# Loading a batch's first pairs ahead of w2, summing a mean on TensorE part by part, spreading the statistics and halving the last store

## The chip, the cores and the metric

The kernel runs on one core of one Trainium2 chip. The metric is device time in microseconds (us). Before: 585.83 us, median of 3 runs (585.38 to 586.06). A profile is one execution; its span is about 1.8 us shorter than the device time of the same execution. Every run also lists its mean granted clock of TensorE (1.0 is full clock).

Names: PE is TensorE, DVE VectorE, ACT ScalarE, POOL GpSimd, SP SyncE. "xT" is the attention output transposed, "xc" the same minus its mean, "ps" the first FFN product, "o_ps" the second, "sc" the scores, "av_ps" attention times v.

## The reference

```python
# q, k, v: (8 batches, 12 heads, 448 tokens, 64); w1: 768 x 3072; w2: 3072 x 768
scores = scale * np.matmul(q, k.transpose(0, 1, 3, 2))
attn = np.maximum(scores, 0.0) ** 2 / S
x = np.matmul(attn, v)                       # then heads side by side: (8, 448, 768)
mu = mean(x); var = mean((x - mu) ** 2)
xn = (x - mu) / sqrt(var + 1e-6) * g_ln
out = x + np.maximum(xn @ w_ch1, 0.0) @ w_ch2
```

## The kernel before

Heads are worked in 6 pairs per batch, numbered through from zero (pair 12 is the first of batch two; some of the expectations say "batch one" for batch zero). Batches zero and one are transposed on PE. From batch two on the transposes of q and k are DMA transposes from the SP queue; q, k, v and the weights come through the POOL queue, which casts to bf16. Batches are taken two by two: FFN one of both, then FFN two of both, with the next batches' attention steps spread between. "warm" matmuls on constant data keep PE busy in the first batch, where there is no FFN to fill it.

```python
def load_paired(b):
    alloc_batch(b)
    for a in range(NPAIR):
        load_pair(b, a)                       # q, q, k, k: 56 KB each
        if a == 1:
            load_heads(b, [("v", 0, H)])      # 672 KB

def att_AV(i, half=None):
    ...
    nc.vector.tensor_scalar(xT_of(b, pr), ps, c2, None, op0=Alu.mult)
    if pr == 1:
        nc.vector.tensor_add(xs[b], xT_of(b, 0), xT_of(b, 1))
    elif 1 < pr < NPAIR - 1:
        nc.vector.tensor_add(xs[b], xs[b], xT_of(b, pr))

def center(b):
    mean_ps = ps_m.tile([P, S], fp32, tag="m")
    nc.tensor.matmul(mean_ps, ones, xs[b], start=True, stop=False)
    nc.tensor.matmul(mean_ps, ones, xT_of(b, K1 - 1), start=False, stop=True)
    ...
    for ki in range(K1):
        nc.vector.tensor_sub(xc_t[:, ki, :], xT_of(b, ki), mean_ps)

def first_end():                              # end of batch zero
    att_AV(NPAIR - 1, 0)
    att_T(NPAIR, evac=False)
    warm_up(4)
    att_AV(NPAIR - 1, 1)
    warm_up(8)
    center(0)
    att_T_out(NPAIR)
...
        for c in range(W2C):                  # order of the POOL queue, after w1
            load_w2(c)                        # 4 x 1152 KB
        load_paired(2)
```

## Time and profile before

| what | value | where |
|---|---|---|
| device time, span | 585.83 us, 583.8 us | runs, page |
| PE busy | 563.6 us | busy times |
| longest wait of PE | 8.9 us, one time | waits |
| from 93 to 578.9 us | PE without a gap | chain of waits |
| last matmul to the end of the span | 4.94 us | timeline |

The waits of PE in the kernel before (who waited for whom, total us, times, longest us):

```profile
PE sc L209 <- DMA qkT_t<-k_sb: 8.9, 1, 8.9
PE ps L290 <- DVE xc_t L257: 1.8, 7, 0.7
```

The chain of work that ended last, around that wait. The profiler follows it back from the last instruction, at each step to what released it (start us, us, what):

```profile
71.23 1.26 PE ps L290 x6
72.48 1.07 SPq L177
...
73.67 7.69 DMA qkT_t<-k_sb
81.36 0.04 issue
81.40 1.00 PE sc L209 x4
82.40 2.35 PE ps L290 x6
...
86.83 2.38 PE ps L290 x12
```

PE stands from 72.5 to 81.4 us for the k transpose of pair 12. The two rows after it are slow: six FFN matmuls take 2.35 us, while later twelve take 2.38. The stretches of ten us (busy time of each engine, granted clock, DMA share, GB/s) show why:

```profile
10.00:20.00 10.00, 9.81 (x108) 4.34 (x105) 9.60 (x18) 9.93 (x13) 5.26 (x7) 1.00 1.37 201
20.00:30.00 10.00, 8.28 (x70) 3.81 (x69) 9.93 (x17) 8.09 (x10) 9.96 (x6) 1.00 1.37 201
...
70.00:80.00 10.00, 2.47 (x18) 0.87 (x14) 3.46 (x10) 2.57 (x4) 6.49 (x9) 0.80 1.49 141
80.00:90.00 10.00, 8.60 (x40) 3.41 (x41) 3.41 (x6) 5.15 (x7) 6.26 (x9) 0.69 2.29 134
```

After the length of the stretch the columns are PE, PEld (weight loads), DVE, ACT, POOL, then the granted clock, the DMA share and GB/s. The clock is 0.69 from 80 to 90 us. From 10 to 30 us DVE (third) is nearly full, and ACT (fourth) from 10 to 20. The end of batch zero on DVE (start us, us, engine, line, what, idle before and its releaser):

```profile
29.57 0.61 DVE L242 TENSOR_SCALAR xT_t<-av_ps 128x448 bf16<-128x448 f32 x1
30.21 0.98 DVE L246 TENSOR_TENSOR xs_t<-xs_t,xT_t 128x448 bf16<-128x448 bf16 x1
31.12 0.61 DVE L212 TENSOR_TENSOR at<-at 112x896 bf16<-112x896 bf16 x1
32.20 0.62 DVE L242 TENSOR_SCALAR xT_t<-av_ps 128x448 bf16<-128x448 f32 x1 [0.47 <-PE av_ps L235]
33.56 3.28 DVE L257 TENSOR_TENSOR xc_t<-xT_t,mean_ps 128x448 bf16<-128x448 bf16 x6 [0.73 <-PE mean_ps L253]
```

The mean addition of 0.98 us stands in front of the last squaring (L212), on which AV and the mean hang.

### The profile page before, as it was taken

What the parts mean: (1) busy time and instruction counts of PE and PEld (TensorE: products, weight loads), DVE (VectorE), ACT (ScalarE), POOL (GpSimd) and SP (SyncE); (2) the same over time, 40 slices, a digit from 0 to 9 for tenths busy, and PEclk for the clock granted to TensorE, in tenths of its full rate; (3) what the DMA queues carried; (4) which work ended last, traced back from release to release, by engine and by line L of the source; (5) the groups of instructions that cost most, each with busy time, mean ns of one, the idle gap of its engine ahead of it and who ended that gap; (6) DMA issues with size and microseconds to landing.
All of it is one profiled execution on the core that took longest, in us unless ns stands there. A gap on an engine that the chain in (4) does not pass through costs nothing.

```text
span 583.8 us, 8969 instructions
## 1 busy us (share of the span) xinstructions
PE 563.6 (97%) x3542; PEld 287.3 (49%) x3542; DVE 263.6 (45%) x505; ACT 266.7 (46%) x392; POOL 143.3 (25%) x188
## 2 busy tenths in 40 slices
PE   8989949999999999999999999999999999999996
PEld 5444414445555444445555544445555544556663
DVE  4977814284544334375444424256454334401111
ACT  6937825672233576663232475664313364440000
POOL 7793170163006500074003610074000000000000
PEclk9999969999999999999999999999999999999999
DMA  9999999299218933599125954299223141000121
GB/s 181 201 205 210 195 145 129 38 116 96 71 44 105 154 36 58 78 111 104 44 71 66 169 54 80 47 95 112 54 58 73 47 71 33 0 2 28 55 54 55
DMA packets 153242, 51.79 MB, mean 89 GB/s; under 512 B 125808, under 2 KB 149616, under 8 KB 153200
## 3 DMA queue, kind: packets, MB, share of 16 engines
q0 software_dynamic: 90144, 25.50, 45.3%
q1 hardware_dynamic: 62576, 25.25, 22.0%
q8 instruction: 28, 0.46, 0.3%
q10 hardware_dynamic: 480, 0.46, 0.3%
q14 instruction: 14, 0.11, 0.1%
HBM read 51.91 MB, written 11.01 MB: 108 GB/s over the span
## 4 chain that ended last, share of the span: by engine, by line
PE 90%; DVE 5%; DMA 2%; ACT 1%; issue 0%; SPq 0%; ACTq 0%
PE o_ps L306 38%; PE ps L290 37%; PE sc L209 7%; PE av_ps L235 6%; DVE at L212 2%; ACT at L211 1%; DMA qkT_t<-k_sb 1%; DVE xc_t L257 1%; DMA h_114<-in_q_dram 1%; DVE qkT_t L201 1%; DVE xT_t L242 0%; DVE xs_t L246 0%; PE tp_ps L190 0%; PE mean_ps L253 0%; PE mean_ps L252 0%
## 5 line engine op out<-in xcount | busy, mean ns | idle before, releaser
L290 PE MATMUL ps<-xc_t,w_112 128*128 128x448 bf16 x1152 | 230.1, 354 | 1.8 <-DVE xc_t L257 1.8
L211 ACT ACTIVATE at<-sc 112x896 bf16<-112x896 f32 x192 | 165.0, 915 | 138.1 <-PE sc L209 137.6
L306 PE MATMUL o_ps<-w_113,h_114 128*128 128x384 bf16 x1344 | 225.6, 326 | 0.0
L212 DVE TENSOR_TENSOR at<-at 112x896 bf16<-112x896 bf16 x192 | 120.2, 632 | 184.2 <-ACT at L211 184.2
L306 PEld LDWEIGHTS <-h_114 128*128 128x128 bf16 x1344 | 128.6, 98 | 95.0 <-issue 12.2
L290 PEld LDWEIGHTS <-w_112 128*128 128x128 bf16 x1152 | 108.7, 98 | 115.6 <-issue 18.8
L292 ACT ACTIVATE h_114<-ps 128x448 bf16<-128x448 f32 x192 | 104.6, 545 | 110.6 <-PE ps L290 110.3
L112 POOL DMA_DIRECT2D q_sb<-in_q_dram x72 | 50.3, 703 | 213.1 <-DMA qkT_t<-q_sb 114.8
L309 DVE SCALAR_TENSOR_TENSOR o_t<-o_ps,rstd_t,x_t 128x384 f32<-128x384 f32 x56 | 34.5, 616 | 82.1 <-PE o_ps L306 82.1
L209 PE MATMUL sc<-qkT_t 64*112 64x448 bf16 x384 | 59.8, 378 | 10.3 <-DMA qkT_t<-k_sb 8.9
L112 POOL DMA_DIRECT2D k_sb<-in_k_dram x72 | 50.2, 701 | 38.8 <-DMA v_sb<-in_v_dram 26.2
L235 PE MATMUL av_ps<-at,v_sb 112*64 112x448 bf16 x384 | 47.3, 361 | 1.0 <-DVE at L212 0.6
L209 PEld LDWEIGHTS <-qkT_t 64*112 64x112 bf16 x384 | 18.4, 126 | 46.4 <-issue 34.3
L257 DVE TENSOR_TENSOR xc_t<-xT_t,mean_ps 128x448 bf16<-128x448 bf16 x48 | 26.2, 614 | 16.2 <-PE mean_ps L253 16.2
L242 DVE TENSOR_SCALAR xT_t<-av_ps 128x448 bf16<-128x448 f32 x48 | 29.6, 617 | 3.6 <-PE av_ps L235 3.6
L235 PEld LDWEIGHTS <-v_sb 112*64 112x64 bf16 x384 | 17.6, 109 | 24.7 <-issue 18.3
L159 POOL TENSOR_SCALAR w_112<-w_112,g_sb 128x512 bf16<-128x512 bf16 x12 | 20.8, 1744 | 1.3 <-DMA w_112<-in_moe_w_ch_dram 1.3
L284 DVE BATCH_NORM_STATS2 stats<-x_t 128x6 f32<-128x384 bf16 x28 | 15.2, 542 | 0.0
L283 DVE BATCH_NORM_STATS2 stats<-x_t 128x6 f32<-128x384 bf16 x28 | 14.6, 523 | 0.0
L327 PE MATMUL w_ps<-w_113,ones 128*128 128x256 bf16 x70 | 11.4, 304 | 1.2 <-DVE w_113 L77 1.2
L279 DVE RECIPROCAL rstd_t<-rstd_t 128x7 f32<-128x7 f32 x4 | 0.8, 201 | 22.5 <-ACT rstd_t L278 22.5
L246 DVE TENSOR_TENSOR xs_t<-xs_t,xT_t 128x448 bf16<-128x448 bf16 x24 | 10.0, 416 | 0.8
(36 smaller groups left out, 81.0 us busy)
## 6 DMA issues: line engine op xcount, KB each, us to landing
v_sb<-in_v_dram POOLq DMA_DIRECT2D x7, 672.0 KB, 10.0
w_112<-in_moe_w_ch_dram POOLq DMA_DIRECT2D x6, 768.0 KB, 25.8
w_113<-in_moe_w_ch_dram POOLq DMA_DIRECT2D x4, 1152.0 KB, 19.1
q_sb<-in_q_dram POOLq DMA_DIRECT2D x72, 56.0 KB, 4.1
k_sb<-in_k_dram POOLq DMA_DIRECT2D x72, 56.0 KB, 4.1
out_dram<-o_t SPq DMA_DIRECT2D x8, 336.0 KB, 2.8
out_dram<-o_t SPq DMA_DIRECT2D x8, 288.0 KB, 2.6
out_dram<-o_t SPq DMA_DIRECT2D x8, 240.0 KB, 2.6
```

The lines of the kernel that those rows point to most:

```text
L112: nc.gpsimd.dma_start(by_pair[:, a, :, x, :], src[b, 2 * a + x].rearrange("(p j) d -> p j d", j=NJ))
L159: eng.tensor_scalar(w, w, g_sb[:, ki:ki + 1], None, op0=Alu.mult)
L209: nc.tensor.matmul(sc[:SP, hh, :S], qkT[i][r, 1, t * SP:(t + 1) * SP], qkT[i][r, 0, :], start=True, stop=True)
L211: nc.scalar.activation(at, sc[:SP, :, :S], Act.Relu)
L212: nc.vector.tensor_mul(at, at, at)
L235: nc.tensor.matmul(ps[hh * D:(hh + 1) * D, :], v_sb[:, 2 * pr + hh, t * D:(t + 1) * D], attn[i, t][:, hh, :], start=(t == 0), stop=(t == N ...
L242: nc.vector.tensor_scalar(xT_of(b, pr), ps, c2, None, op0=Alu.mult)
L257: nc.vector.tensor_sub(xc_t[:, ki, :], xT_of(b, ki), mean_ps)
L290: nc.tensor.matmul(ps, w1[:, ki, ni * P:(ni + 1) * P], xc[u * U + bb][:, ki, :], start=(ki == 0), stop=(ki == K1 - 1))
L292: nc.scalar.activation(h1[:, ni, bb * S:(bb + 1) * S], ps, Act.Relu)
L306: nc.tensor.matmul(o_sb[1], h1[:, ki, m * P:(m + 1) * P], w2[:, ki, j * hd:(j + 1) * hd], start=(ki == 0), stop=(ki == K2 - 1))
L309: nc.vector.scalar_tensor_tensor(o_sb[0][:, j * hd:(j + 1) * hd], o_sb[1], rstd[u][:, m:m + 1], x_tok[u][:, m, j * hd:(j + 1) * hd], op0=A ...
```

## The change

Four parts with different aims: get pair 12 and 13 in before w2, so that PE needn't stand; take the additions for batch zero's mean off DVE, with PE summing part by part in place of warm-up matmuls; run the statistics every second FFN block over the last 14, in place of every block of the last 7; and store the last tile in two column halves, so that less is left after the last matmul.

```diff
-    def load_paired(b):
-        alloc_batch(b)
-        for a in range(NPAIR):
+    def load_paired(b, a0=0, a1=NPAIR):
+        if a0 == 0:
+            alloc_batch(b)
+        for a in range(a0, a1):
...
+        if b == 0:
+            return                            # no additions on DVE for batch zero
         if pr == 1:
             nc.vector.tensor_add(xs[b], xT_of(b, 0), xT_of(b, 1))
...
+    def mean_part(ki):
+        if ki == 0:
+            mean0_ps = ps_f.tile([P, S], fp32, tag="f")
+            mean0[0] = mean0_ps
+        nc.tensor.matmul(mean0[0], ones, xT_of(0, ki), start=(ki == 0), stop=(ki == K1 - 1))
...
+            last = u == NU - 1 and m == MU - 1
-            if j == 1:
+            if j == 1 or last:
+                d0, d1 = (j * hd, (j + 1) * hd) if last else (0, d_model)
...                                           # store columns d0:d1
-        warm_up(4)
+        if i > 1:
+            mean_part(i - 2)
+            warm_up(2)
+        else:
+            warm_up(4)
...                                           # first_end: the same, mean_part(NPAIR - 2)
-                if bb == 1 and ni >= K2 - MU:
-                    items.append((0.0, lambda u=u, m=ni - (K2 - MU): ffn_stats(u, m)))
+                m = (ni - (K2 - 2 * MU)) // 2
+                if bb == 1 and m >= 0 and ni % 2 == 0:
+                    items.append((0.0, lambda u=u, m=m: ffn_stats(u, m)))
...
+        load_paired(2, 0, 2)
         for c in range(W2C):
             load_w2(c)
-        load_paired(2)
+        load_paired(2, 2)
```

More of the change, by code (lines that the diff above doesn't have):

```diff
@@ L43 @@
     MU = UT // P
+    NU = B // U
     assert SP * NJ == S and MU * P == UT
@@ L226, in att_AV @@
                 xT[b // U] = xT_t
-            xs_t = xs_pool.tile([P, S], bf16, tag="xs")
-            xs[b] = xs_t
+            if b > 0:
+                xs_t = xs_pool.tile([P, S], bf16, tag="xs")
+                xs[b] = xs_t
         if half != 1:
@@ L248 @@
     xc = {}
-    def center(b):
-        mean_ps = ps_m.tile([P, S], fp32, tag="m")
-        nc.tensor.matmul(mean_ps, ones, xs[b], start=True, stop=False)
+    mean0 = {}
+    def mean_part(ki):
[3 more added lines that the diff above has]
+        nc.tensor.matmul(mean0[0], ones, xT_of(0, ki), start=(ki == 0), stop=(ki == K1 - 1))
+    def center(b):
+        if b == 0:
+            mean_ps = mean0[0]
+        else:
+            mean_ps = ps_m.tile([P, S], fp32, tag="m")
+            nc.tensor.matmul(mean_ps, ones, xs[b], start=True, stop=False)
         nc.tensor.matmul(mean_ps, ones, xT_of(b, K1 - 1), start=False, stop=True)
@@ L318, in ffn_2 @@
                     nc.sync.dma_start(
-                        out_tok[u * U + bb, c0 - g0 * SP:c1 - g0 * SP, jj, :],
-                        o_sb[0][c0 - m * P:c1 - m * P, :])
+                        out_tok[u * U + bb, c0 - g0 * SP:c1 - g0 * SP, jj, d0:d1],
+                        o_sb[0][c0 - m * P:c1 - m * P, d0:d1])
                     c0 = c1
@@ L367, in step_fine @@
         att_QK(i, 3)
-        warm_up(4)
+        if i > 1:
+            mean_part(i - 2)
+            warm_up(2)
+        else:
+            warm_up(4)
     def first_end():
@@ L372, in first_end @@
         att_T(NPAIR, evac=False)
-        warm_up(4)
+        mean_part(NPAIR - 2)
+        warm_up(2)
         att_AV(NPAIR - 1, 1)
@@ L398, in steps_of @@
         return done_at[b]
-    NU = B // U
     segs = []
```

## The prediction

> **What bounds it now.** TensorE is busy 563.6 of 583.8 us (busy times). Its waits sum to 14.8 us, 8.9 of them one wait of the score matmul (L209) for the DMA transpose of k. From 93 to 578.9 us the chain of waits is TensorE without a gap. Three places can give time:
>
> 1. **Stall at 72.5 to 81.4 us (chain, timeline).** Batch two's first q/k loads queue behind w2: w2 lands at 54.5 to 71.5 us, the pairs at 71.9 to 74.5 (issue records); the transposes are issued at 72.3 and 73.7 and land at 76.9 and 81.4, the second slowed by the v load. Then the granted clock is 0.69 for 80 to 90 us (windows): six FFN matmuls took 2.35 us in place of 1.24, four score matmuls 1.00 in place of 0.52; with the next groups about 2.2 us. [...] At stake: 11.1 us.
> 2. **First batch, 8 to 33 us.** The chain is on VectorE (DVE), busy 9.6 and 9.9 of 10 us in 10-20 and 20-30. On it: four mean additions (three of 0.39 us, one 0.98; 2.15 together) and the first mean matmul (0.19).
> 3. **Tail.** Last matmul ends 578.9; DVE 0.62; last store landed 582.7; end 583.8.
>
> **What the change does.**
> - *Loads.* Pairs 12, 13 and v go ahead of w2. From the queue's rates (w1 landed at 48.9; pairs 150 KB/us, v 180, w2 207) I estimate pairs landed by 51, v 56, w2 78, the rest 86. w2 is first used at about 113 then, pair 14 at 91: room for both. Pair 12's transposes are then issued when the program reaches them, at about 56.5, needed at about 70, but beside w2. Beside v they took 7.3 to 10.4 us, alone 2.4. ([...] the trace shows the transposes nearly silent for 3.5 us while v was served.) w2's pieces take 131 ns against 61, so I estimate landing at 65 to 72: a stall of 0 to 3 us remains, about 1. Gain about 10.
> - *Mean.* Four DVE additions leave the chain; five matmuls of 0.19 us replace ten warm-up matmuls of about 0.12 in TensorE's slack. ScalarE idled 1.25 us before its last activation there, but DVE is the longer: gain about 2.2.
> - *Statistics spread.* No TensorE wait comes from them: 0.
> - *Store by halves.* The final store carries half; from 2.8 us to landing, about 0.5.
>
> Sum: about 12.9 us. **Predicted 572.9 us, 8 in 10 between 571.0 and 576.5; faster by over 2% 0.68, within 2% 0.31, slower 0.01.**
>
> **What would show each step.** (1) The 8.9 us wait gone or under 3; granted clock 0.95 or more from 70 to 90 us; w2 landing at 72 to 79. (2) First FFN matmul at about 31.9 in place of 34.2. (3) TensorE waits unchanged around the statistics. (4) Last matmul to end 4.4 us in place of 4.9.
>
> **What would make it wrong.** Transposes starved for all of w2 (clock drop again: 577 to 580). ScalarE binding in the first batch (gain 1). Statistics ahead of the sixth x transpose's landing, blocking DVE and then TensorE. A PSUM wait because the running mean holds one of two "f" buffers.

Passages that no trace or run of this case shows are cut out of it, and out of the expectations of "changed, again" and "four warm-ups" below, where marked. About 10 for the loads, 2.2 for the mean, 0 and about 0.5 come to 12.7, and "about 12.9" was recorded (585.8 less 572.9).

## The result

The changed kernel took 572.41 us (572.13 to 573.27, 4 runs) against 585.82 us (4 runs). The ratio is 0.9774, 95% interval 0.9758 to 0.9791. A ratio here is the mean time of one kernel's fast runs over that of the other's in the same rounds, so it is not quite the ratio of the medians quoted. The ratio is clear of 2% here and when the kernel ran a third time; in the second (0.9781, interval up to 0.9801) it just isn't.

The longest waits of PE in the changed kernel; the wait for the k transpose is gone:

```profile
PE ps L306 <- DVE xc_t L273: 1.8, 7, 0.7
PE w_ps L345 <- DVE w_113 L78: 1.2, 1, 1.2
PE tp_ps L192 <- DVE xT_t L245: 0.7, 1, 0.7
```

The timeline of PE where it stood before, and that of the SP queue which issues pair 12's and 13's transposes:

```profile
70.44 1.31 PE L306 MATMUL ps<-xc_t,w_112 128*128 128x448 bf16 x6
71.68 0.58 PE L211 MATMUL sc<-qkT_t 64*112 64x448 bf16 x4
72.20 1.31 PE L306 MATMUL ps<-xc_t,w_112 128*128 128x448 bf16 x6
```

```profile
58.22 1.29 SPq L179 DMA_TRANSPOSE qkT_t<-q_sb  x1
59.62 1.24 SPq L179 DMA_TRANSPOSE qkT_t<-k_sb  x1
64.14 1.19 SPq L179 DMA_TRANSPOSE qkT_t<-q_sb  x1
65.44 1.30 SPq L179 DMA_TRANSPOSE qkT_t<-k_sb  x1
```

The transposes are issued at 58.2 and 59.6 us in place of 72.3 and 73.7. By the issue records they land at 67.5 and 71.6 us, the second 0.06 us before the score matmul that needs it starts. The stretches:

```profile
20.00:30.00 10.00, 9.19 (x89) 4.10 (x88) 8.86 (x15) 7.57 (x9) 9.97 (x6) 1.00 1.37 201
30.00:40.00 10.00, 8.38 (x51) 3.52 (x51) 6.91 (x13) 2.85 (x5) 8.83 (x7) 0.83 1.30 206
70.00:80.00 10.00, 9.84 (x60) 4.45 (x57) 7.72 (x16) 7.14 (x11) 1.40 (x2) 1.00 1.17 203
80.00:90.00 10.00, 9.85 (x58) 4.47 (x57) 4.08 (x8) 6.80 (x11) 5.47 (x8) 1.00 1.51 149
```

From 70 to 90 us the clock is full now. But it is 0.83 between 30 and 40 us, where it was 1.00 in the profile of before. On DVE the end of batch zero now reads:

```profile
27.75 0.61 DVE L245 TENSOR_SCALAR xT_t<-av_ps 128x448 bf16<-128x448 f32 x1
28.29 0.61 DVE L214 TENSOR_TENSOR at<-at 112x896 bf16<-112x896 bf16 x1
30.06 0.62 DVE L245 TENSOR_SCALAR xT_t<-av_ps 128x448 bf16<-128x448 f32 x1 [1.16 <-PE av_ps L238]
31.22 3.28 DVE L273 TENSOR_TENSOR xc_t<-xT_t,mean_ps 128x448 bf16<-128x448 bf16 x6 [0.54 <-PE mean_ps L269]
```

The addition is gone, but DVE now waits 1.16 us for AV, where it waited 0.47.

To compare many profiles I read three marks from each trace: A, the start of the first score matmul; B, the start of the sixth matmul of the first FFN group (the last one to wait for centring); C, the end of the last matmul. All in us:

| kernel | A | B | A to B | B to C | C to end |
|---|---|---|---|---|---|
| before | 7.13 | 36.89 | 29.76 | 541.96 | 4.94 |
| changed | 6.83 | 34.55 | 27.71 | 532.74 | 4.21 |

So this pair of profiles gives 2.3 us up to B, 9.2 us from B to C (with the halved clock near 35 us in it) and 0.7 us in the tail: 12.3 us, the difference of the spans (583.8 less 571.5). The first two were then tested by runs; the tail was only read from the traces. The last PE row of each timeline, before and changed, ends at 578.85 and 567.28 us:

```profile
574.79 4.06 PE L306 MATMUL o_ps<-w_113,h_114 128*128 128x384 bf16 x24
565.82 1.46 PE L322 MATMUL o_ps<-w_113,h_114 128*128 128x384 bf16 x8
```

### The profile page after: what moved, and what is told of

It reads as the page before. It is cut to its first block, busy times and chain, and to the rows that moved or that the text cites. A ratio compares the mean times of both kernels' runs of the same rounds, so it can differ in the third digit from the quotient of the medians.

```text
span 571.5 us, 8962 instructions
## 1 busy us (share of the span) xinstructions
PE 562.1 (98%) x3536; PEld 286.4 (50%) x3536; DVE 261.8 (46%) x501; ACT 266.1 (47%) x392; POOL 144.4 (25%) x188
## 4 chain that ended last, share of the span: by engine, by line
PE 93%; DVE 4%; ACT 2%; DMA 1%; issue 0%; SPq 0%; ACTq 0%
PE o_ps L322 39%; PE ps L306 38%; PE sc L211 8%; PE av_ps L238 7%; ACT at L213 2%; DVE at L214 1%; DVE xc_t L273 1%; DMA h_114<-in_q_dram 1%; PE tp_ps L192 0%; DVE qkT_t L203 0%; DVE xT_t L245 0%; PE w_ps L345 0%; PE mean_ps L269 0%; PE mean_ps L268 0%; DVE o_t L325 0%
## 5 line engine op out<-in xcount | busy, mean ns | idle before, releaser
L325 DVE SCALAR_TENSOR_TENSOR o_t<-o_ps,rstd_t,x_t 128x384 f32<-128x384 f32 x56 | 34.5, 616 | 82.1 <-PE o_ps L322 82.1
L345 PE MATMUL w_ps<-w_113,ones 128*128 128x256 bf16 x60 | 10.0, 303 | 1.2 <-DVE w_113 L78 1.2
L102 POOL DMA_DIRECT2D v_sb<-in_v_dram x10 | 9.0, 897 | 1.1 <-issue 0.8
```

The source lines that it names most:

```text
L325: nc.vector.scalar_tensor_tensor(o_sb[0][:, j * hd:(j + 1) * hd], o_sb[1], rstd[u][:, m:m + 1], x_tok[u][:, m, j * hd:(j + 1) * hd], op0=A ...
```

## The experiments

Twelve runs were made in three calls (loads only to changed, again; all pairs first to long piece; changed, third to statistics only), each call on another chip; "before" is from the runs of the same call.

| kernel | time us (median, range) | runs | before us | ratio | 95% interval |
|---|---|---|---|---|---|
| loads only | 574.76 (573.06 to 576.04) | 4 | 585.96 | 0.9807 | 0.9785 to 0.983 |
| mean only | 585.61 (585.19 to 586.55) | 5 | 585.96 | 0.9997 | 0.9984 to 1.001 |
| no mean | 573.58 (572.86 to 573.87) | 4 | 585.96 | 0.9787 | 0.9773 to 0.98 |
| changed, again | 573.77 (571.9 to 574.52) | 5 | 585.96 | 0.9781 | 0.9761 to 0.9801 |
| all pairs first | 572.7 (572.29 to 572.76) | 4 | 586.84 | 0.9764 | 0.975 to 0.9778 |
| four warm-ups | 572.51 (572.32 to 574.4) | 4 | 586.84 | 0.977 | 0.9751 to 0.9788 |
| real filling | 572.12 (571.89 to 572.55) | 5 | 586.84 | 0.9757 | 0.9743 to 0.9771 |
| filling, pairs, long piece | 571.88 (571.4 to 572.34) | 4 | 586.84 | 0.9752 | 0.9737 to 0.9767 |
| changed, third | 572.84 (572.25 to 573.73) | 4 | 586.35 | 0.9768 | 0.9753 to 0.9783 |
| end order | 572.33 (571.57 to 572.68) | 4 | 586.35 | 0.9756 | 0.9742 to 0.9771 |
| best | 571.54 (571.51 to 571.94) | 4 | 586.35 | 0.9746 | 0.9732 to 0.9761 |
| statistics only | 586.14 (586.12 to 586.62) | 4 | 586.35 | 0.9996 | 0.9979 to 1.0013 |

All outputs are right.

### Loads only

The kernel before with only the last hunk of the diff and its `load_paired`.

```diff
+        load_paired(2, 0, 2)
         for c in range(W2C):
             load_w2(c)
-        load_paired(2)
+        load_paired(2, 2)
```

> The kernel before with the load order alone changed (pairs 12 and 13 and v ahead of w2). Theory A (the load order carries most of the gain by itself, because it removes the 8.9 us wait and the halved clock after it): about 10.8 us under before, some 575.0 us, no wait of L209 for a transpose over 1 us. Theory B (the load order only pays together with the shorter first batch): under 8 us.

It took 574.76 us, ratio 0.9807: 11.2 us by the medians, no wait of PE for a transpose over 0.2 us, and B to C is 531.21 us in place of 541.96. Theory A holds. The 10.75 us between the two are the 8.9 us of the wait and most of the 2.2 us of slow clock.

Two of its four executions had a mean clock of 0.998 and 1.0 (573.75 and 573.06 us), the other two 0.996 and 0.995 (576.04 and 575.77). The profile is of the first kind, so where the other two lost 2.5 us is not on record. This kernel still adds the mean on DVE and has all its warm-ups; that will matter below.

### Mean only

The kernel before with the mean hunks only.

> The kernel before with the mean of batch one summed on TensorE alone. Theory A (the time won in the first batch is lost again, because the first score matmul of batch two must wait for loads whose landing is set by the DMA queue and not by VectorE): within 0.5 us of before, and the wait for the transpose of k grows from 8.9 to about 11 us. Theory B (the terms add up): about 2.2 us under before, 583.6 us, wait unchanged at 8.9.

The time did not move (0.9997). The wait of PE grew:

```profile
PE sc L211 <- DMA qkT_t<-k_sb: 10.9, 1, 10.9
```

Its first batch ended earlier (B at 35.06 in place of 36.89), and the score matmul of pair 12 still started at 81.55 us; in the kernel before at 81.40, with the statistics only at 82.05. With the loads late, DMA sets this start, and what the first batch wins is given back here. Theory A holds, but not all of the growth from 8.9 to 10.9 us comes from the mean part: statistics only, with the additions on DVE, waited 10.5 us, since its first batch too ended earlier than in the profile of before (B at 36.01).

### The mean with the loads early, and the changed kernel again

"No mean" is the changed kernel with the mean hunks taken back.

> The changed kernel without the mean part: load order, statistics and halved last store. If the mean is worth 2.2 us once the loads are early: 2.2 us over the changed kernel, about 574.5 us. If the halved clock at 34.6 to 38.0 us in the changed kernel's profile is what the mean part costs every time: only 0.7 us over it. No halved clock near 35 us is expected here, since the warm-up matmuls are those of before.

> The changed kernel again. Theory A (the halved clock for 3.4 us in the first profile is one execution's luck [...]): most executions have mean granted clock 1.0 and lie about 1 us under those that have not, near 572.2 against 573.3. Theory B (the cut of ten warm-up matmuls causes it in every execution): granted clock 0.996 in all. If a profile with full clock is caught: first FFN matmul at 31.9 us, a small wait, up to 1.5 us, of L209 for the transpose of k may show, since it landed only just in time in the first profile.

> The changed kernel once more, as the measure for the others of this call and to count its clock states: some executions at granted clock 0.998 to 1.0 with spans of 570.1 to 570.8, some at 0.996 to 0.997 with spans of 571.5 to 572.7. From the first FFN matmul group's sixth matmul to the last matmul: 531.2 us at full clock, 532.7 with the halved window. From the first score matmul to that sixth matmul: 27.7 to 28.5 us.

No mean took 573.58 us and the changed kernel beside it 573.77: no gain to be seen. Sorted by their granted clock, the 13 executions of the changed kernel fall apart: eight at 0.998 or more took 571.90 to 572.91 us (mean 572.38), five at 0.997 or less took 573.27 to 574.52 (mean 573.86). No mean (four at 0.998 or 0.999, mean 573.47) lies 1.1 us above the first group. So neither expectation of 2.2 us over nor of 0.7 us is met as stated; the worth is up to 1.1 us at full clock. Even that is generous: between the profiles of no mean and of the changed kernel's third run the spans differ by 1.08 us, of which 0.63 lie before A, where no part of the mean has run.

The five executions at 0.997 or less lost 1.5 us. The mean part isn't shown to cause this, since two of the four executions of loads only, which lacks that part, show a low clock too.

The marks of all profiles show where the 2.2 went:

| kernel | A to B | last of ACT's 24 activations, from A | from there to xc | B to C |
|---|---|---|---|---|
| before | 29.76 | 22.22 | 4.21 | 541.96 |
| statistics only | 28.39 | 21.12 | 3.94 | 543.32 |
| loads only | 28.24 | 20.93 | 3.97 | 531.21 |
| no mean | 28.57 | 21.27 | 3.97 | 531.16 |
| mean only | 27.95 | 21.08 | 3.53 | 544.23 |
| changed | 27.71 | 20.88 | 3.51 | 532.74 |
| changed, again | 28.07 | 21.20 | 3.53 | 532.71 |
| changed, third | 28.12 | 21.26 | 3.53 | 531.15 |
| four warm-ups | 28.07 | 21.30 | 3.44 | 531.18 |
| all pairs first | 28.46 | 21.03 | 4.10 | 531.16 |

The upper four add the mean on DVE, the lower six on PE (the last two kernels are told of below). ACT needs 21 us for its 24 activations either way. The kernel before was profiled in an execution in which ACT happened to be held up (22.22); in loads only, which adds on DVE as before does, ACT runs through. ACT's timelines in the kernel before and in loads only:

```profile
7.57 15.26 ACT L211 ACTIVATE at<-sc 112x896 bf16<-112x896 f32 x18
23.02 1.74 ACT L211 ACTIVATE at<-sc 112x896 bf16<-112x896 f32 x2 [0.19 <-DVE at L212]
25.09 2.61 ACT L211 ACTIVATE at<-sc 112x896 bf16<-112x896 f32 x3 [0.33 <-PE sc L209]
28.43 0.92 ACT L211 ACTIVATE at<-sc 112x896 bf16<-112x896 f32 x1 [0.73 <-PE sc L209]
```

```profile
7.97 20.50 ACT L212 ACTIVATE at<-sc 112x896 bf16<-112x896 f32 x24 [0.58 <-PE sc L210]
```

Only what comes after ACT's last activation is shorter, by 0.44 us (3.97 to 3.53) in most profiles. All pairs first is the exception: there DVE's last four squarings before the end took 3.04 us in place of 2.63 in the changed kernel's third profile, so DVE was still behind, and its A to B is no shorter than with the additions on DVE. Why this execution of before lost 1.2 us of ACT's time and others did not is open.

### The halved clock near 35 us: four warm-ups, and real work as filling

Between 31 and 34.5 us PE has only six FFN matmuls, each waiting for its part of xc. The stretch in which the clock is halved and the one before it, in the first profile of the changed kernel:

```profile
31.14:34.56 3.42, 1.80 (x7) 0.49 (x6) 3.34 (x7) 0.00 (x0) 3.42 (x3) 1.00 1.32 204
34.56:37.97 3.41, 3.41 (x11) 1.12 (x10) 1.98 (x4) 1.14 (x3) 2.24 (x3) 0.50 1.24 207
```

In the clock records the granted clock of the first profile is 1.0 for 30.72 us, then 0.50 for 3.413 us, then 1.0 for 532.48; in the kernel before 1.0 for 71.68, 0.50 for 10.24 and 1.0 for 494.93. All six are whole multiples of the shortest, 3.413 us: 9, 1, 156 and 21, 3, 145 (the records after the last matmul are left out). In the second profile the halving starts 30.72 us after the first grant again. So I count steps of 3.413 us from the first grant. The step before the halving is 31.14 to 34.56 us in the first profile, with PE busy 1.80 us, and 31.96 to 35.37 us in the second, with 1.87; in the kernel before it lies in the stall, 72.56 to 75.97 us, with none. In the third profile, where no halving came, the first grant is at 5.04 us, and the steps are 28.94 to 32.35 and 32.35 to 35.76 us, with 2.77 and 2.38 us busy. So in these three profiles of the changed kernel the halving came where most of the idle fell into one step, and the steps fall differently from one profile to the next. What decides it is not shown, and a busy time at which it comes can't be read off: in the profile of best the step from 4.70 to 8.11 us had 1.80 us busy too, and no halving followed.

> The changed kernel with the warm-up matmuls back at four beside each part of the mean. Theory A (the halved clock near 35 us comes from the idle of TensorE while the mean is subtracted, 31 to 34.5 us, [...]; the warm-ups before do not matter): still some executions at granted clock 0.996, some at 1.0, spans as the changed kernel. Theory B (the cut of warm-ups causes it): all executions at 1.0.

```diff
             mean_part(i - 2)
-            warm_up(2)
+            warm_up(4)
```

(The same in `first_end`.) One of four executions still had 0.996 and 574.4 us, the others 572.32 to 572.62. So the number of warm-ups is not the cause, if this execution was halved in the same place; it was not the one profiled. Loads only, with all its warm-ups, says the same.

> The changed kernel with real work put into the idle of TensorE during the centring of batch one: the transposed q/k of pair 6 copied out by VectorE before the last AV (where VectorE waits), then the first two score matmuls of pair 6 and the transposes of pair 7 right after the mean matmul, ahead of the first FFN group. Theory A (idle in the centring halves the clock at times): all executions at clock 1.0, and 0.5 to 0.9 us of TensorE work leaves the path; but the score matmul of pair 12 then meets the floor of its transpose, so little of it is seen: 0 to 0.5 us under full-clock executions of the changed kernel, median about 572.0. Theory B: no change of the clock pattern.

```diff
-        att_T(NPAIR, evac=False)
+        att_T(NPAIR)
...
         center(0)
-        att_T_out(NPAIR)
+        step_a(NPAIR)
+        att_T(NPAIR + 1)
...
-            att.append(lambda i=i: (step_a(i), att_T(i + 1)))
```

All five executions had 0.998 or more. Counting the two later kernels with this filling, 13 of 13 were free of it, while of 33 with the early loads and the idle left in (the changed kernel's 13, loads only, no mean, four warm-ups, all pairs first, end order) 8 had 0.997 or less. But five of the eight fell in the first call, in which no kernel with the filling ran; in the other two it was 2 of 16 against 0 of 13 (the eighth is of the first measurement). And only two of the eight were profiled. In these two the halving followed the idle in centring; that the filling prevents it is not shown. The 0.9 us of work moved forward gave nothing: B to C is 531.19, as in the changed kernel at full clock, though less work is left after B. In its place PE's waits for ACT grew:

```profile
PE sc L211 <- ACT at L213: 1.0, 6, 0.2
```

They were 0.5 us in three waits in the changed kernel's third profile. That ACT paces the stretch from 35 to 70 us is argued from this, not shown by a run of its own.

### How near the transpose is: all pairs first, end order

> The changed kernel with all six pairs of batch two ahead of w2 (not only the first two). Theory A (beside w2 one piece of a transpose is served for one piece of w2, 134 ns to 31, so the k transpose of pair 12 lands at about 71.5 us whatever the first batch does, and this is a floor that eats about 1.2 us of the mean's gain in executions with full clock): the transposes of pair 12, beside pieces of 128 bytes that take 31 ns, land by 64 us, and full-clock executions drop about 1.2 us under those of the changed kernel (spans 570.1 to 570.8), to about 569.2. w2 lands at about 90 us, long before its use at 113. Theory B (no stall is left): within 0.3 us of the changed kernel at the same clock.

```diff
-        load_paired(2, 0, 2)
+        load_paired(2)
         for c in range(W2C):
             load_w2(c)
-        load_paired(2, 2)
```

The transposes of pair 12 landed at 62.3 and 64.3 us, as expected. But the time did not fall (572.7 us, all at 0.999 or 1.0), and B to C stayed at 531.16. The theory of a floor under the changed kernel fell: its transpose lands just in time, not late. The DMA mix that I had blamed is real, though. In the changed kernel the queues' packets from 63 to 79 us, while pairs 12 and 13 are transposed beside w2:

```profile
q0 software_dynamic: 1840, 2.77, 94.8%
q1 hardware_dynamic: 1834, 0.44, 22.0%
```

(Columns: packets, MB, share of 16 engines.) The engines served one packet of the transposes (q1, 256 bytes, 31 ns) for each one of w2 (q0, 1536 bytes, 134 ns). By my estimate a transpose of 448 packets therefore takes about 4 us, at 1834 packets in 16 us. The first one was issued at 58.2 us and had its first packet at 62.2. From issue to landing the four took 9.3 to 14.5 us; in the kernel before it was 7.3 to 10.4 beside a v load, and 2.4 alone (issued at 99.0 and 100.3).

> The changed kernel with one order changed at the end of batch one: the last AV half ahead of the fifth part of the mean and its warm-up matmuls. Theory A (after the mean left VectorE, the path there is TensorE in order: transposes held by a PSUM buffer, mean part, two warm-ups, then AV; VectorE waits 1.16 us for AV): VectorE's wait shrinks to about 0.6 us, first score matmul to sixth FFN matmul about 27.5 in place of 28.0, time about 0.5 us under the changed kernel at the same clock. Theory B (ScalarE's 24 activations set the end alone): no change.

```diff
         att_T(NPAIR, evac=False)
-        mean_part(NPAIR - 2)
-        warm_up(2)
         att_AV(NPAIR - 1, 1)
-        warm_up(8)
+        mean_part(NPAIR - 2)
+        warm_up(6)
```

DVE's wait shrank as expected, and centring starts 0.63 us earlier than in the changed kernel's third profile (31.17 in place of 31.80):

```profile
30.03 0.62 DVE L245 TENSOR_SCALAR xT_t<-av_ps 128x448 bf16<-128x448 f32 x1 [0.52 <-PE av_ps L238]
31.17 3.27 DVE L273 TENSOR_TENSOR xc_t<-xT_t,mean_ps 128x448 bf16<-128x448 bf16 x6 [0.52 <-PE mean_ps L269]
```

A to B is 27.33. So 0.6 us more was blocked by PE's own order: AV stood behind the transposes, a mean part and two warm-ups. But the profile then shows a new wait:

```profile
PE sc L211 <- DMA qkT_t<-k_sb: 1.0, 1, 1.0
```

and the chain of waits in the same stretch:

```profile
57.93 12.16 DMA qkT_t<-k_sb
70.10 0.04 issue
70.14 0.42 PE sc L211 x2
```

B to C is 532.21, 1.0 us more. Here the floor is reached: the transpose took 12.16 us beside w2. That is the remaining stall the prediction had feared, and the changed kernel escapes it only because its first batch is slower. By the medians end order is 0.5 us under the changed kernel of the same call (572.33 and 572.84), with overlapping ranges. At full clock little is left: its four executions have a mean of 572.23 us, the changed kernel's eight 572.38.

### Statistics and last store

> The kernel before with the statistics spread alone. Theory A (no TensorE wait hangs on them): within 0.3 us of before, TensorE waits as before, 8.9 us for the transpose of k; VectorE may stand for some us in front of the sixth x transpose without effect. Theory B: over 1 us either way.

The ratio is 0.9996. After the first batch PE's waits changed only in the one for the k transpose (10.5 us, see mean only). In the changed kernel DVE does stand in front of the sixth x transpose, and PE has no wait for it:

```profile
104.85 0.56 DVE L300 BATCH_NORM_STATS2 stats<-x_t 128x6 f32<-128x384 bf16 x1 [7.69 <-DMA x_t<-xT_t]
```

The halved store had no run of its own. From the last matmul to the end of the span it is 4.94 to 4.99 us in the four profiles without it and 4.18 to 4.21 in those with it: 0.75 us. In time this was not seen by itself: loads only and no mean, which differ in the statistics and the store, took 573.06 and 573.75 us (its two at full clock) and 573.47 (mean of four).

> Real work in the centring, all pairs ahead of w2, and the last tile's long piece of rows (112) stored before its short one (16). If the floor of pair 12's transpose held back both others: the sum, about 1.2 + 0.7 + 0.35 us under full-clock executions of the changed kernel, span about 568.2, time about 570.0. If not: near the better of the two singles.

Storing the last tile's 112-row piece before its 16-row piece brought that to 3.89 us, 0.3 us less. The sum that was expected (570.0 us) was not reached, since the filling and the pairs gave nothing: 571.88 us.

### A version that beats both

End order (with five warm-ups at the end in place of six), real filling, and the long piece first.

> The new order, real work in the centring (against the halved clock) and the last tile's long piece stored first. Sum against full-clock executions of the changed kernel: 0.5 to 0.6 by the order, 0.3 by the store, nothing more by the filling but no execution with a halved window: span about 569.5, time about 571.2, below both kernels.

It took 571.54 us (571.51 to 571.94), ratio 0.9746. The changed kernel in the same rounds took 572.84 (572.25 to 573.73); the ranges don't meet (in the first call, though, the changed kernel had one execution of 571.90). No execution was under 0.999. Of the 0.42 us between the two profiles 0.30 lie in the tail, by the long piece, and 0.16 before B; B to C is 531.19, as before. All pairs first together with end order was not run; the 1.0 us wait above says that it could give something.

## Why the prediction was right

The time was predicted as 572.9 us and measured as 572.41, and the reason given first carried it. But the terms of the sum were not equally good.

- **Loads: about 10, measured 10.8 to 12.1.** The wait and the slow clock are gone, as predicted; loads only shows that this part stands alone. The lower figure takes the profile of before for B to C, the upper that of statistics only (543.32 less 531.21), whose load order is the same and whose first batch ended earlier, so that PE waited longer. The transposes landed at 67.5 and 71.6, within the predicted 65 to 72. The remaining stall of about 1 us did not come in the changed kernel, but did as soon as the first batch was 0.6 us shorter. One detail missed: w2 was complete at 84.1 us, not 72 to 79, since the estimate did not charge w2 for the transposes beside it. Its first use is at 114.7, so it cost nothing.
- **Mean: 2.2, measured at most 1.1.** This step was mis-sized. The prediction took the chain of waits of one execution for the rule ("DVE is the longer: gain about 2.2"). The first profile seemed to confirm it (first FFN matmul at 31.9, as predicted), but other profiles of the same kernel have 32.5 and 32.6, and kernels with the additions on DVE reach 33.1 to 33.6 (all pairs first, with the mean on PE, 32.9). ACT's 24 activations take 21 us in all but the one profile I had, so the case listed under what would make it wrong, ScalarE binding with a gain of 1, is what the runs show. Then PE's order took part of the rest.
- **Halved clock: not foreseen.** 1.5 us in 5 of 13 executions, about 0.6 us on average; two of them were profiled, and there it lay in centring.
- **Statistics: 0, measured 0** (0.9996, interval 0.9979 to 1.0013).
- **Store: 0.5, measured 0.75.**

In the first profile pair these terms gave 12.3 us, with one halved stretch of 3.41 us; the timed runs, three of four at full clock, gave 13.4 by the medians. Between the profile of before and the third of the changed kernel, at full clock, the spans differ by 13.3 us: 0.1 up to A, 1.6 from A to B, 10.8 from B to C, 0.75 in the tail. About 1 us of the 1.6 is not the mean's: it is what ACT was held up in the one profile of before. Where ACT was not held up (statistics only), the wait for the transpose was longer instead, so this time belongs to the loads. The loads were put 1 to 2 us too low and the mean 1 to 2 us too high. That the total was nearer than its parts is in part luck.

## What to carry to other kernels

Order the loads of a shared queue by when they are needed, not by size: a 224 KB pair behind 4.6 MB of weights cost 8.9 us and a halved clock (0.50 for 10.24 us), and undoing it was worth more than all else. A part's worth depends on what holds the next meeting point: with the pairs late the shorter first batch was worth nothing, with them early 0.4 to 1.1 us, and a further 0.6 us met the transpose again. When two engines are both near full, the chain of waits of one execution does not tell which of them sets the pace; look at the slower engine's own gaps in several profiles before counting an addition as saved.
